# Delta-rule attention followed by a mixture of experts: group preparation, expert 0's first slots and expert 1's split moved in the order

## Chip, cores and metric

The kernel runs on one core of a Trainium2 chip. The metric is the device time of one launch in microseconds (us), as the median of runs; the time before is 915.78 us, of 3 runs. The program has two halves that follow one another: attention, in 24 units, and a mixture of 8 experts.

## What is computed

The first half is a recurrence over 768 steps for each of 4 x 8 heads, with a 40 x 40 state; the second sends each of the 3072 rows of its result to 2 of 8 experts. Cut to what matters:

```python
for t in range(S):                                   # 768 steps, state 40 x 40 per head
    y[:, :, t] = einsum('bhd,bhde->bhe', rt, state)
    Sa = einsum('bhde,bhe->bhd', state, at)
    state = state * wt - einsum('bhd,bhe->bhde', Sa, bt) + einsum('bhd,bhe->bhde', vt, kt)
x = y as 3072 rows of 320
noisy = x @ w_gate + log1p(exp(x @ w_noise)) * noise  # 3072 x 8
top2, top2_w = the two largest of 8, softmax over the two
for e in range(8):                                   # w1[e] is 320 x 1024, w2[e] is 1024 x 320
    out[rows of e] += weight * (relu(x[rows of e] @ w1[e]) @ w2[e])
```

## The kernel before

**Attention.** The 768 steps are cut into 12 chunks of 64; half of the batch (p = 0 or 1) in one chunk is a unit, so 24 units, each of which writes one tile of 128 rows (`run`, `for n in range(N+1)`). Four units with two chunks form a group g (units 4g to 4g+3). Before a group can run, it is prepared, inside the units of the groups before it (`prep`): loads of w, a and k/b (`loadw`, `loada`, `loadq`), a scan on DVE with its logarithm and exponential on ACT (`scan`, `lnexp`), the factor NH on DVE (`newton`), products on POOL that write A (`mula`, am) and KB (`mulk`, bm and km), 64 matmuls and an eviction (`prepS`, L: tiles lt and No; `prepK`, K: tile ak), transposes of KB (`quad`). lt goes to DRAM (scr) by `flush`, comes back as X (`Solve`), POOL solves 16 x 16 triangles in it in 14 pairs of operations on X and Tt (`step`), it is written to DRAM again (`done`) and comes back as XD (`fetchD`, fD), in two chunks. A table of events (`ev(unit, slot, function)`) says in which unit and in which slot of the unit's body each step is issued; `do(n,slot)` issues them.

A unit's body is a chain that PE runs through in order: pkb of the unit before (tile YS), xdt (pX, from XD), state (pd, WS), mm1, the last unit's result (pg), umm, mmx (px) three times with DVE's H and dT between, ut (pU), rmm (sc from RV, VU; DVE writes PV), akv, rnmm. All compute instructions of this half go through a wrapper that chains each engine's instructions in program order, so their line in the profile is L443, the wrapper's. DMAs of SP are chained likewise. Every engine takes its queue in order: an instruction that waits holds all behind it.

**Route.** The rows' logits come with pg (DVE's lg). After 8, 8, 4, 2 and 2 tiles (`RTS`) a generator `route` computes the gate, ranks and slots in small steps; each of the six `adv` calls of a unit runs one step and one scatter (POOL's indirect DMA ls<-ent,po, one for each tile and rank). cnt on DVE feeds pr on PE (counts of rows before), pr feeds po, the slots. Rows of the first `NA` = 20 tiles go to the list ls[0] and the rows xd[0], later ones to copies ls[1], xd[1]; `turn` copies the list.

**Experts.** An expert has 832 slots in two parts (`PARTS`): 0 to 511, filled from the first 20 tiles for expert 0, and 512 to 831. `loadx` reads the list of a part (le, by SP) and gathers rows (xr, POOL's indirect DMA per 128 rows), `trans` turns them on PE (pt) and splits them into two f16 halves (xh on ACT, xl and x3l on DVE), `split1` and `split2` do so with the weights (w1h, w1l, w2h, w2l), `hidden` makes 8 blocks of 8 matmuls (ph; hh on ACT, hl on DVE), `output` 24 matmuls for each 128 slots (po; y on ACT), which POOL adds to the output. `sized` and `finite` are reductions on DVE (mx, yc) for a flag. For the experts the order comes from a scheduler, except where `pin` sets an operation behind another of the same engine (`marks`); the splits of expert 0 are pinned to places in the units, those of expert 1 behind the last instruction of the units (`s.end`), and mx<-xr is free.

Of the kernel before, what the change touches and what calls it, by code (L numbers as in the profile page):

```python
# [17 lines left out]
R=104  # L18
# [4 lines left out]
NA=20  # L23
# [8 lines left out]
PARTS=((0,512),(512,CAP-512))  # L32
# [12 lines left out]
class Moe:  # L45
# [81 lines left out]
    def route(s,n0,T,lg):  # L127
# [9 lines left out]
        yield 1  # L137
        pr=s.rps[0].tile([128,T,8],F32,name="pr",tag=s.rps[1],bufs=s.rps[2])
# [146 lines left out]
    def trans(s,x,e,X=None,part=0):  # L285

        nc=s.nc; xp=s.xps[e%2]
        if X is None:
            X=[xp.tile([128,2,s.cap],F16,name="xh"),xp.tile([128,2,s.cap],F16,name="xl"),
               xp.tile([128,s.cap],F16,name="x3"),xp.tile([128,s.cap],F16,name="x3l")]  # L290
        xh,xl,x3,x3l=X
        t0,n=s.parts[part]; t0%=CAP
        for k in range(3):
            pt=s.pt.tile([128,512],F32,name="pt",bufs=2)
            f0=min(128*k,DM-128)
            for t,p in tiles(t0,n): nc.tensor.transpose(pt[:,t-t0:t-t0+p],x[:p,t//128,f0:f0+128],s.idm[:p,:p])  # L296
            r=slice(t0,t0+n)
            if k<2:
                nc.scalar.activation(xh[:,k,r],pt[:,:n],AF.Copy,scale=XE)  # L299
                nc.vector.scalar_tensor_tensor(xl[:,k,r],pt[:,:n],XE,xh[:,k,r],op0=ALU.mult,op1=ALU.subtract)  # L300
            else:
                for q in (slice(0,64),slice(64,128)): nc.scalar.activation(x3[q,r],pt[64:128,:n],AF.Copy,scale=XE)
                for q in (slice(0,64),slice(64,128)): nc.vector.scalar_tensor_tensor(x3l[q,r],pt[64:128,:n],XE,x3[64:128,r],op0=ALU.mult,op1=ALU.subtract)
        return X
    def hidden(s,W,X,part):
        nc=s.nc; wh,wl=W; xh,xl,x3,x3l=X
        t0,n=s.parts[part]; t0%=CAP; r=slice(t0,t0+n)
        hh=s.hp.tile([128,8,n],F16,name=f"hh{part}"); hl=s.hp.tile([128,8,n],F16,name=f"hl{part}")
        for f in range(8):
# [170 lines left out]
class Att:  # L480
    def __init__(s,nc,tc,ctx,aps):
# [5 lines left out]
        s.No=[own(f"No{i}",[128,2,CG*4,64]) for i in range(4)]; s.XDT=own("XDT",[128,8,64])  # L487
        s.ak=[own(f"ak{i}",[128,2,CG*4,64]) for i in range(2)]
        s.MT=own("MT",[128,2,4,64]); s.XD=[own(f"XD{i}",[128,4,2,2,64]) for i in range(2)]; s.H1=own("H1",[128,2,4,64]); s.H2=own("H2",[128,2,4,64])
        s.A=[own(f"A{(i+2*NG)%SAB}",[128,NS,64]) for i in range(SAB)]; s.A=[s.A[(i-2*NG)%SAB] for i in range(SAB)]  # L490
        s.Gx=[own(f"Gx{i}",[R,NS,64]) for i in range(SAB)]; s.ge=[own(f"ge{i}",[R,NS,1]) for i in range(SAB)]
        s.kbt=[own(f"kbt{i}",[128,CG*640+24]) for i in range(4)]
# [206 lines left out]
    def run(s,m,xo=None):  # L699
# [62 lines left out]
        def prep(g):  # L762
# [10 lines left out]
            ev(n-7,'f1',lambda: (scan(g,0),am(g,0)))  # L773
            ev(n-7,'a1',lambda: ln(g,0)); ev(n-7,'a2',lambda: ex(g,0))
# [10 lines left out]
            ev(n-3,'f1',lambda: sol[g].step(Pl,15))  # L785
            ev(n-2,'f2',lambda: done(g,Pl))
# [3 lines left out]
        def finish(o,n):  # L790
            xt,lg=s.rows(o)
            if m is not None: m.logits(n,xt,lg)
            else: nc.sync.dma_start(xo[o['p'],o['cc']],xt)
        for n in range(N+1):
# [41 lines left out]
            do(n,'s3')  # L836
# [133 lines left out]
```

## Time and profile before

| | us |
|---|---|
| median of 3 runs | 915.78 |
| lowest, highest | 911.03, 918.65 |
| the profiled execution, its own time | 919.16 |
| its span, first to last instruction | 917.4 |
| PE busy | 771.6 (84%) |
| DVE, POOL, ACT busy | 485.5, 383.4, 332.8 |

Times in the profile count from the start of the span. A row of the timeline has start, length, engine, line, operation, out<-in, shapes, the count of merged instructions, and in brackets how long the engine sat idle before and what ended that. PE is matmuls, PEld its weight loads, SPq the queue of SP that issues DMAs. A row of the windows has the stretch, its length, busy time and count of PE, PEld, DVE, ACT and POOL, then the mean granted TensorE clock (1.0 is 2.4 GHz, 0.5 is 1.2 GHz), the share of the DMA engines and GB/s. In the list of waits stand total us, times, longest. Unit 4 begins at about 146 us, unit 23 at about 490 us, the experts behind 514 us.

### The profile page before, as it was taken

What the parts mean: (1) busy time and instruction counts of PE and PEld (TensorE: products, weight loads), DVE (VectorE), ACT (ScalarE), POOL (GpSimd) and SP (SyncE); (2) the same over time, 40 slices, a digit from 0 to 9 for tenths busy, and PEclk for the clock granted to TensorE, in tenths of its full rate; (3) what the DMA queues carried; (4) which work ended last, traced back from release to release, by engine and by line L of the source; (5) the groups of instructions that cost most, each with busy time, mean ns of one, the idle gap of its engine ahead of it and who ended that gap; (6) DMA issues with size and microseconds to landing.
All of it is one profiled execution on the core that took longest, in us unless ns stands there. A gap on an engine that the chain in (4) does not pass through costs nothing.

```text
span 917.4 us, 28566 instructions
## 1 busy us (share of the span) xinstructions
PE 771.6 (84%) x12521; PEld 591.7 (65%) x12521; DVE 485.5 (53%) x959; ACT 332.8 (36%) x684; POOL 383.4 (42%) x496
## 2 busy tenths in 40 slices
PE   0063798998798998898984599999999999999994
PEld 0043687887787887787873346566666666666663
DVE  6372464654674654653563754775656565654231
ACT  3021343443343442342432324544444353533230
POOL 9031453263279563256223337525251526141313
PEclk9985898999898997999897589999999999999997
DMA  8942364755765764657595325717171717130303
GB/s 156 187 88 58 82 153 115 159 146 137 186 159 102 150 161 93 165 126 173 131 266 151 105 59 108 192 50 185 27 189 21 191 27 183 38 41 8 40 9 44
DMA packets 164393, 106.81 MB, mean 116 GB/s; under 512 B 116847, under 2 KB 147443, under 8 KB 163971
## 3 DMA queue, kind: packets, MB, share of 16 engines
q1 hardware_dynamic: 152099, 87.75, 39.1%
q0 software_dynamic: 12160, 17.15, 10.8%
q8 instruction: 100, 1.64, 0.8%
q14 instruction: 34, 0.28, 0.1%
HBM read 80.16 MB, written 28.10 MB: 118 GB/s over the span
## 4 chain that ended last, share of the span: by engine, by line
PE 65%; DMA 11%; POOL 10%; DVE 5%; issue 4%; SPq 3%; ACT 1%; POOLq 0%; ACTq 0%
PE ph L314 20%; PE po L328 19%; PE sc L443 6%; PE YS L443 6%; PE px L443 4%; POOL X L443 3%; PE WS L443 3%; PE pt L296 2%; DMA scr<-X 2%; PE pg L443 2%; DMA scr<-lt 2%; SPq L443 2%; POOL Tt L443 2%; DMA X<-scr 2%; DMA XD<-scr 2%
## 5 line engine op out<-in xcount | busy, mean ns | idle before, releaser
L337 POOL DMA_INDIRECT out_dram<-y,le x48 | 80.0, 1667 | 183.0 <-ACT y L331 180.2
L316 DVE SCALAR_TENSOR_TENSOR hl<-ph,hh 128x320 f16<-128x320 f32 (+1 forms) x128 | 74.6, 589 | 72.1 <-ACT hh L315 71.1
L315 ACT ACTIVATE hh<-ph 128x320 f16<-128x320 f32 (+1 forms) x128 | 65.6, 516 | 127.2 <-PE ph L314 125.7
L314 PEld LDWEIGHTS <-w1h 128*128 128x128 f16 x768 | 74.4, 99 | 57.4 <-issue 6.1
L328 PEld LDWEIGHTS <-hh 128*128 128x128 f16 (+1 forms) x1024 | 84.2, 101 | 37.0 <-issue 3.7
L443 POOL TENSOR_TENSOR KB<-KB,NH 104x1024 f32<-104x1024 f32 x20 | 47.5, 2399 | 99.9 <-DMA KB<-in_fm_dram 56.6
L443 PE MATMUL sc<-A,KB 64*64 64x64 f32 x1536 | 34.6, 245 | 53.1 <-DVE mk L511 20.0
L328 PE MATMUL po<-w2h,hh 128*128 128x320 f16 (+1 forms) x512 | 74.3, 284 | 0.2 <-ACT hh L315 0.2
L283 POOL DMA_INDIRECT xr<-xd,le x56 | 54.3, 969 | 36.4 <-DMA le<-ls 17.1
L314 PE MATMUL ph<-xh,w1h 128*128 128x512 f16 (+1 forms) x256 | 66.8, 345 | 3.1 <-ACT xh L299 3.1
L328 PE MATMUL po<-w2h,hl 128*128 128x320 f16 (+1 forms) x512 | 68.3, 282 | 0.0
L328 PE MATMUL po<-w2l,hh 128*128 128x320 f16 (+1 forms) x512 | 67.7, 282 | 0.0
L314 PE MATMUL ph<-xh,w1l 128*128 128x512 f16 (+1 forms) x256 | 67.2, 343 | 0.0
L314 PE MATMUL ph<-xl,w1h 128*128 128x512 f16 (+1 forms) x256 | 66.6, 342 | 0.0
L443 PEld LDWEIGHTS sc<-A,KB 64*64 64x64 f32 x1536 | 30.9, 156 | 54.4 <-issue 26.5
L443 DVE TENSOR_TENSOR H<-px,XD 128x512 f32<-128x512 f32 x48 | 33.2, 691 | 61.8 <-PE px L443 61.0
L331 ACT ACTIVATE y<-po,le 128x320 f32<-128x320 f32 (+1 forms) x56 | 28.3, 505 | 87.6 <-PE po L328 87.6
L227 DVE TENSOR_REDUCE yc<-y 128x1 f32<-128x320 f32 (+1 forms) x56 | 25.3, 460 | 54.9 <-ACT y L331 54.6
L443 POOL DMA_INDIRECT ls<-ent,po x44 | 47.9, 1088 | 9.5 <-issue 8.0
L328 PEld LDWEIGHTS <-hl 128*128 128x128 f16 (+1 forms) x512 | 42.4, 101 | 14.6
L443 PE MATMUL sc<-RV,VU 64*128 64x64 f32 x768 | 50.2, 282 | 0.9 <-ACT VU L443 0.7
L443 ACT ACTIVATE kbt<-ptr 128x320 f32<-128x320 f32 x48 | 20.9, 436 | 82.4 <-PE ptr L443 82.4
(261 smaller groups left out, 1591.9 us busy)
## 6 DMA issues: line engine op xcount, KB each, us to landing
w2r<-in_w_dram SPq DMA_DIRECT2D x7, 1280.0 KB
w1r<-in_w_dram SPq DMA_DIRECT2D x7, 1024.0 KB
KB<-in_fm_dram SPq DMA_DIRECT2D x32, 208.0 KB
w1r<-in_w_dram SPq DMA_DIRECT2D x20, 256.0 KB
RV<-in_rv_dram SPq DMA_DIRECT2D x24, 208.0 KB
VU<-in_rv_dram SPq DMA_DIRECT2D x24, 208.0 KB
V<-in_vt_dram SPq DMA_DIRECT2D x24, 160.0 KB
PV<-in_vt_dram SPq DMA_DIRECT2D x48, 80.0 KB
```

Source lines behind the costliest of these rows:

```text
L227: s.pin(s.nc.vector.tensor_reduce(s.yc[q:128,s.ny:s.ny+1],a,axis=AX.X,op=ALU.add),0); s.ny+=1
L283: for k in range(c,c+a): nc.gpsimd.indirect_dma_start(out=x[:p,k],out_offset=None,in_=s.xd[w],in_offset=OFFS(ap=li[:p,k,0:1],axis=0))
L296: for t,p in tiles(t0,n): nc.tensor.transpose(pt[:,t-t0:t-t0+p],x[:p,t//128,f0:f0+128],s.idm[:p,:p])
L314: for i,(a,b) in enumerate(mm): nc.tensor.matmul(ph[:,:n],a,b,start=i==0,stop=i==7)
L315: nc.scalar.activation(hh[:,f],ph[:,:n],AF.Relu)
L316: nc.vector.scalar_tensor_tensor(hl[:,f],ph[:,:n],0.0,hh[:,f],op0=ALU.max,op1=ALU.subtract)
L328: for j in range(c): nc.tensor.matmul(po[p*j:p*j+p,:d],h[:,f,r],w[:,f,d*j:d*j+d],start=k==0,stop=k==23)
L331: nc.scalar.activation(y[:,:d],po[:,:d],AF.Copy,scale=w_[:,ii:ii+1])
L337: st=nc.gpsimd.indirect_dma_start(out=o_,out_offset=OFFS(ap=ix,axis=0),in_=yv,in_offset=None,compute_op=ALU.add)
L443: i=f(*a,**kw)
```

## The change

1. The preparation of groups 2 to 5 is moved: the loads are packed into fewer units (six slots, s0 to s5); L stands in a new slot `L` behind the result of the last unit, its eviction and `flush` right behind it; NH, bm and km of the first half at the end of unit 4g-6, of the second at the end of unit 4g-5; the solver's load and its steps in unit 4g-4, `done` at the end of unit 4g-3; scan and NH stand behind the first mmx or at the unit's end, not at its start. fD goes from behind the third mmx to the unit's start from unit 4 on. Group 1 keeps its slots.
2. `route` has one more step between cnt and pr.
3. `NA` is 16 and part 0 has 384 slots, part 1 has 448. The list and rows of expert 0's part 0 are read in unit 20 (`early`), turned and split in units 22 and 23 (`trans1`), into tiles of their own.
4. mx<-xr, the reductions of expert 0's w1l and w1h, and expert 1's splits of w1 are pinned behind the last route's po (`s.placed`) and between the hh and hl of expert 0.
5. Some tiles change places in SBUF.

```diff
-NA=20
+NA=16
-PARTS=((0,512),(512,CAP-512))
+PARTS=((0,384),(384,CAP-384))
...
         cnt=r("cnt",dt=F16); nc.vector.tensor_tensor(cnt,oh[:,:,0],oh[:,:,1],op=ALU.add)
         yield 1
+        yield 1
...
-        s.mark(8); s.finite(l.rearrange("p k f->p (k f)")); s.mark(10); s.finite(h[64:128,2],64)
+        s.w1=lambda: (s.mark(8),s.finite(l.rearrange("p k f->p (k f)")),s.mark(10),s.finite(h[64:128,2],64))
+        if e: s.w1()
...
+    def early(s):
+        n=PARTS[0][1]//128; l=s.kp.tile([128,n,4],F32,name="le0"); x=s.kp.tile([128,n,DM],F32,name="xr0")
+        li=l.rearrange("p a f->p (a f)").bitcast(I32).rearrange("p (a f)->p a f",a=n)
+        s.x0=s.loadx(0,(x,l[:,:,2],li[:,:,1:2],l,li),0); s.X0=s.xtiles(s.kp,PARTS[0][1],"0")
...
         with s.tc.high_priority(offset=PX):
-            x=s.loadx(0); W1=s.split1(r1,0); X=s.trans(x[0],0)
-            s.sized(x[0][:,0])
-        W2=s.split2(r2,0); H0=s.hidden(W1,X,0)
+            W1=s.split1(r1,0)
+        W2=s.split2(r2,0); H0=s.hidden(W1,s.X0,0); hm=s.hm
...
             H1=s.hidden(W1,X,1)
+            if e==0: s.at=s.placed,; s.sized(s.x0[0][:,0]); s.marks=[s.at]*12; s.w1(); s.at=None; s.marks=[(s.placed,hm[k][1]) for k in (4,4,5,5,6,6,7,7,7,7,7,7)]+[s.hm[k] for k in (2,2,3,3,4,4)]
...
-                for u,l in ((n-8,(None,w_(0,0),w_(0,1),la(0,0))),(n-7,(la(0,1),w_(1,0),w_(1,1),lq(0,0))),
-                            (n-6,(lq(0,1),lq(0,2),lq(0,3),la(1,0))),(n-5,(la(1,1),lq(1,0),lq(1,1),lq(1,2))),(n-4,(lq(1,3),))):
+                for u,l in ((n-8,(w_(0,0),w_(0,1),la(0,0),la(0,1),w_(1,0),w_(1,1))),(n-7,(None,)*5+(lq(0,0),)),
+                            (n-6,(lq(0,1),lq(0,2),lq(0,3),la(1,0),la(1,1),lq(1,0))),(n-5,(lq(1,1),lq(1,2),lq(1,3)))):
...
-            ev(n-6,'f1',lambda: nh(g,0))
-            ev(n-5,'f1',lambda: (bm(g,0),km(g,0),scan(g,1)))
-            ev(n-5,'f2',lambda: am(g,1))
-            ev(n-5,'a1',lambda: ln(g,1)); ev(n-5,'a2',lambda: ex(g,1))
-            ev(n-5,'sc',lambda: L(g,0))
-            ev(n-4,'f1',lambda: (nh(g,1),bm(g,1),km(g,1)))
-            ev(n-4,'sc',lambda: L(g,1)); ev(n-3,'ld2',lambda: sol_(g))
+                ev(n-6,'f1',lambda: nh(g,0)); ev(n-6,'p4',lambda: (bm(g,0),km(g,0)))
+                ev(n-5,'L',lambda: L(g,0)); ev(n-5,'fl',s.flush)
+                ev(n-5,'f1',lambda: (scan(g,1),am(g,1)))
+                ev(n-5,'p2',lambda: ln(g,1)); ev(n-5,'a1',lambda: ex(g,1))
+                ev(n-5,'p4',lambda: (nh(g,1),bm(g,1),km(g,1)))
+                ev(n-4,'L',lambda: L(g,1)); ev(n-4,'fl',s.flush)
+                ev(n-4,'p3',lambda: sol_(g)); ev(n-4,'p4',lambda: sol[g].step(Pl,15))
+                ev(n-3,'p4',lambda: done(g,Pl))
...
-            ev(n-3,'f1',lambda: sol[g].step(Pl,15))
-            ev(n-2,'f2',lambda: done(g,Pl))
...
+        def late(n): return n<6
...
+            if not late(n+2): fD(n+2)
...
+                if n==EX: m.early()
+                if n==EX+2: m.trans1(m.x0[0],m.X0,0,0,s.ps,"pB",1)
+                if n==EX+3: m.trans1(m.x0[0],m.X0,0,2,s.ps,"pB",1)
...
+            if m is not None and n==EX+2: m.trans1(m.x0[0],m.X0,0,1,s.ps,"pA",1)
...
+EX=20
```

On SP's queue, the last group's way from X to XD, before:

```order
L443 DMA X<-scr 128x1024
L443 DMA PV_266<-in_vt_dram 64x8x40 x2
L443 DMA xd_651<-xt 128x320
L443 DMA RV_261<-in_rv_dram 104x512
L443 DMA VU_263<-in_rv_dram 104x8x64
L443 DMA V_264<-in_vt_dram 128x320
L443 DMA PV_267<-in_vt_dram 64x8x40 x2
L443 DMA xd_651<-xt 128x320
L443 DMA scr_6143<-X 128x1024
L443 DMA XD_133<-scr_6143 32x16x32 x4
```

The same on SP's queue in the changed kernel (xd is the row store, RV, VU, V and PV are the inputs of later units):

```order
L450 DMA X<-scr 128x1024
L450 DMA RV_260<-in_rv_dram 104x512
L450 DMA VU_262<-in_rv_dram 104x8x64
L450 DMA V_265<-in_vt_dram 128x320
L450 DMA PV_266<-in_vt_dram 64x8x40 x2
L450 DMA xd_652<-xt 128x320
L450 DMA scr_5900<-X 128x1024
L450 DMA RV_261<-in_rv_dram 104x512
L450 DMA VU_263<-in_rv_dram 104x8x64
L450 DMA V_264<-in_vt_dram 128x320
L450 DMA PV_267<-in_vt_dram 64x8x40 x2
L450 DMA XD_209<-scr_5900 32x16x32 x4
```

X is read one set of a unit's inputs earlier, and the solved block is written and read back with a set between, where XD followed the write at once.

On DVE's queue in unit 23, before, from the gate's wq to cnt:

```order
L443 TENSOR_TENSOR wq<-l_7261 128x2
L224 TENSOR_REDUCE mx<-xr 128x1
L443 TENSOR_TENSOR PV_267<-sc,mk 128x8x64 x2
L443 TENSOR_SCALAR wq<-wq 128x2
L443 RECIPROCAL ent<-wq 128x2
L443 TENSOR_TENSOR ent<-wq,ent 128x2
L443 CAST xf<-ix 128x4
L443 TENSOR_TENSOR oh<-io,xf 128x32
L443 TENSOR_SCALAR ent<-ent 128x4
L443 TENSOR_TENSOR cnt<-oh 128x16
```

The same place on DVE in the changed kernel (x3l is the third split of expert 0's part 0):

```order
L450 TENSOR_TENSOR PV_267<-sc,mk 128x8x64 x2
L450 SCALAR_TENSOR_TENSOR x3l_6708<-pt,x_6707 64x384 x2
L450 TENSOR_SCALAR wq<-wq 128x2
L450 RECIPROCAL ent<-wq 128x2
L450 TENSOR_TENSOR ent<-wq,ent 128x2
L450 CAST xf<-ix 128x4
L450 TENSOR_TENSOR oh<-io,xf 128x32
L450 TENSOR_SCALAR ent<-ent 128x4
L450 TENSOR_TENSOR cnt<-oh 128x16
```

The reduction mx<-xr is gone from there, two x3l have come.

On PE where the units end, before (pg is the last unit's result, pt the transposes of expert 0):

```order
L443 MATMUL pg<-IW,yT 128x120 x4
L296 MATMUL pt<-idm,xr 128x128 x8
L314 LDWEIGHTS w1h
L314 MATMUL ph<-xh,w1h 128x512
L314 LDWEIGHTS w1h
L314 MATMUL ph<-xh,w1h 128x512
```

The same on PE in the changed kernel:

```order
L450 MATMUL pg<-IW,yT 128x120 x4
L321 LDWEIGHTS w1h
L321 MATMUL ph<-xh_6705,w1h 128x384
L321 LDWEIGHTS w1h
L321 MATMUL ph<-xh_6705,w1h 128x384
L321 LDWEIGHTS w1h
```

The first hidden matmuls follow pg without a transpose between.

## Rows read from the trace of the kernel before

**Rows 1.** Page, part 2: PE busy tenths and granted TensorE clock in 40 slices.

```profile
PE   0063798998798998898984599999999999999994
...
PEclk9985898999898997999897589999999999999997
```

**Rows 2.** Chain of waits, the experts: start us, length us, what, instructions.

```profile
797.98 16.72 PE po L328 x158
...
844.83 16.72 PE po L328 x158
861.55 5.29 PE ph L314 x24
...
890.00 15.52 PE po L328 x149
```

**Rows 3.** Windows: three units, full and slowed; columns as in the section above.

```profile
247.20:264.60 17.40, 17.20 (x421) 15.63 (x421) 12.36 (x49) 7.50 (x17) 7.69 (x20) 0.84 0.55 136
264.60:279.80 15.20, 14.45 (x414) 13.04 (x412) 9.22 (x22) 5.19 (x13) 13.31 (x27) 1.00 0.71 162
279.80:300.40 20.60, 16.66 (x414) 14.90 (x412) 8.70 (x18) 8.21 (x17) 19.14 (x21) 0.83 0.46 96
```

**Rows 4.** List of waits of PE, 90 to 515 us, then timeline of PE.

```profile
PE pX L443 <- DMA XD<-scr: 14.9, 5, 4.2
...
145.55 0.63 PE L443 MATMUL pX<-idf,XD 128*128 128x128 f32 x4 [2.98 <-DMA XD<-scr]
...
247.19 1.09 PE L443 MATMUL pX<-idf,XD 128*128 128x128 f32 x4 [4.17 <-DMA XD<-scr]
```

**Rows 5.** Timeline of PE: single waits in units 11, 14 and 21.

```profile
293.21 1.11 PE L443 MATMUL ptr<-idf,KB 128*128 128x128 f32 x4 [3.72 <-POOL KB L443]
...
338.23 0.60 PE L443 MATMUL pU<-idf,Up 128*128 128x128 f32 x4 [1.58 <-DVE H L443]
...
467.79 0.19 PE L443 MATMUL pr<-cnt,tri 128*128 128x32 f16 x1 [2.95 <-DVE cnt L443]
```

**Rows 6.** Timeline of unit 23: the gather, its reader, pr and pg.

```profile
500.26 0.99 POOL L283 DMA_INDIRECT xr<-xd,le  x1 [11.80 <-DMA le<-ls]
...
504.05 0.48 DVE L224 TENSOR_REDUCE mx<-xr 128x1 f32<-128x320 f32 x1 [11.76 <-DMA xr<-xd,le]
...
506.78 0.20 PE L443 MATMUL pr<-cnt,tri 128*128 128x16 f16 x1 [10.92 <-DVE cnt L443]
...
511.89 2.06 PE L443 MATMUL pg<-IW,yT 104*128 104x120 f32 x8 [0.78 <-DVE yT L443]
```

**Rows 7.** Timeline from the last pg to part 1's first gather.

```profile
514.43 2.95 ACT L253 ACTIVATE w1h<-w1r 128x1024 f16<-128x1024 f32 x3
...
519.89 2.72 PE L314 MATMUL ph<-xh,w1h 128*128 128x512 f16 x6 [3.07 <-ACT xh L299]
...
537.84 0.16 DVE L156 SCALAR_TENSOR_TENSOR po<-pf,junk 128x4 int32<-128x4 f32 x1
...
542.14 0.97 POOL L167 DMA_INDIRECT ls<-ent,po  x1 [0.30 <-issue]
...
546.62 0.99 POOL L283 DMA_INDIRECT xr<-xd,le  x1 [3.51 <-DMA le<-ls]
```

**Rows 8.** Timeline: DVE's split and reduction, and a scatter beside them.

```profile
517.00 1.21 DVE L254 SCALAR_TENSOR_TENSOR w1l<-w1r,w1h 128x1024 f16<-128x1024 f32 x1
517.08 2.00 POOL L443 DMA_INDIRECT ls<-ent,po  x1 [0.16 <-issue]
...
520.38 2.28 DVE L227 TENSOR_REDUCE yc<-w1l 128x1 f32<-128x2048 f16 x1
```

**Rows 9.** Timeline: third gather of part 1 and its transposes.

```profile
549.19 0.93 POOL L283 DMA_INDIRECT xr<-xd,le  x1 [0.30 <-issue]
...
553.69 1.16 PE L296 MATMUL pt<-idm,xr 128*128 128x128 f32 x6
```

**Rows 10.** Page, part 5: the products that POOL writes to KB.

```profile
L443 POOL TENSOR_TENSOR KB<-KB,NH 104x1024 f32<-104x1024 f32 x20 | 47.5, 2399 | 99.9 <-DMA KB<-in_fm_dram 56.6
```

More of the change, by code (lines that the diff above doesn't have):

```diff
@@ L267, in split2 @@
         s.mark(17); s.sized(w[:,0])
-        s.at=None; s.marks=[s.end]*18 if e==0 else []
+        s.at=None; s.marks=[]
         return h,l
@@ L287, in trans @@
         nc=s.nc; xp=s.xps[e%2]
[L288 to L291, printed above, removed]
-        t0,n=s.parts[part]; t0%=CAP
[L293 to L303, printed above, removed]
@@ L304, in trans, with xtiles, trans1 @@
-        return X
+        if X is None: X=s.xtiles(xp,s.cap,"")
+        for k in range(3): s.trans1(x,X,part,k,s.pt,"pt",2)
+        return X
+    def xtiles(s,xp,n,z):
+        return [xp.tile([128,2,n],F16,name="xh"+z),xp.tile([128,2,n],F16,name="xl"+z),xp.tile([128,n],F16,name="x3"+z),xp.tile([128,n],F16,name="x3l"+z)]
+    def trans1(s,x,X,part,k,pool,tag,bufs):
+        nc=s.nc; xh,xl,x3,x3l=X
+        t0,n=s.parts[part]; t0%=CAP
+        pt=pool.tile([128,512],F32,name="pt",tag=tag,bufs=bufs)
+        f0=min(128*k,DM-128)
+        for t,p in tiles(t0,n): nc.tensor.transpose(pt[:,t-t0:t-t0+p],x[:p,t//128,f0:f0+128],s.idm[:p,:p])
+        r=slice(t0,t0+n)
+        if k<2:
+            nc.scalar.activation(xh[:,k,r],pt[:,:n],AF.Copy,scale=XE)
+            nc.vector.scalar_tensor_tensor(xl[:,k,r],pt[:,:n],XE,xh[:,k,r],op0=ALU.mult,op1=ALU.subtract)
+        else:
+            for q in (slice(0,64),slice(64,128)): nc.scalar.activation(x3[q,r],pt[64:128,:n],AF.Copy,scale=XE)
+            for q in (slice(0,64),slice(64,128)): nc.vector.scalar_tensor_tensor(x3l[q,r],pt[64:128,:n],XE,x3[64:128,r],op0=ALU.mult,op1=ALU.subtract)
@@ L486, in __init__, with pair, five @@
         s.KB=[own(f"KB{i}",[128,NS,2,64]) for i in range(2)]
[L487 removed]
+        s.No,s.kbt,s.A,s.Gx,s.ge={},{},{},{},{}
+        def pair(i): s.No[i]=own(f"No{i}",[128,2,CG*4,64]); s.kbt[i]=own(f"kbt{i}",[128,CG*640+24])
+        def five(i): s.A[i]=own(f"A{i}",[128,NS,64]); s.Gx[i]=own(f"Gx{i}",[R,NS,64]); s.ge[i]=own(f"ge{i}",[R,NS,1])
+        l=2*((NG-1)%2); z=[(2*NG-2+p)%SAB for p in range(2)]
+        for i in range(4):
+            if i//2*2!=l: pair(i)
+        for i in range(2,SAB): five((i+z[0])%SAB)
+        for i in range(2): pair(l+i)
+        for i in z: five(i)
+        s.No,s.kbt=[[d[i] for i in range(4)] for d in (s.No,s.kbt)]; s.A,s.Gx,s.ge=[[d[i] for i in range(SAB)] for d in (s.A,s.Gx,s.ge)]
+        s.XDT=own("XDT",[128,8,64])
         s.ak=[own(f"ak{i}",[128,2,CG*4,64]) for i in range(2)]
         s.MT=own("MT",[128,2,4,64]); s.XD=[own(f"XD{i}",[128,4,2,2,64]) for i in range(2)]; s.H1=own("H1",[128,2,4,64]); s.H2=own("H2",[128,2,4,64])
[L490 to L492 removed]
         s.wk=ec(tc.tile_pool(name="wk",bufs=2))
@@ L793, in finish, with ld @@
             else: nc.sync.dma_start(xo[o['p'],o['cc']],xt)
+        def late(n): return n<6
+        def ld(n,k):
+            for i in do(n,'s%d'%k):
+                if k in (2,3,4): s.tc.add_manual_dep(i.ins,nc.scalar.last,mybir.DependencyInfo(mybir.DependencyClass.Sync,mybir.DependencyReason.DATA),reason="pace")
         for n in range(N+1):
@@ L802, in run @@
                 finish(r,n-1)
-                if m is not None: m.scatter(99); m.end=(V.last,nc.scalar.last)
+                if m is not None: m.scatter(99); m.end=(V.last,nc.scalar.last,nc.tensor.last)
                 break
             G=Gof(n); first=o['cc']==0; w1=s.w1[n%2]; x=O[n+1] if n+1<N else None
-            do(n,'f1'); adv(1)
+            adv(1)
             s.unit(o,G)
@@ L817, in run @@
             if x: s.mmx(x,0)
+            for f in z: f()
+            do(n,'f1')
             s.ut(o)
+            ld(n,2); do(n,'p2')
             adv(1)
@@ L822, in run @@
             s.rmm(o)
+            do(n,'f3')
             adv(0)
             if x: s.akv(x,Gof(n+1))
+            ld(n,3); do(n,'p3')
             do(n,'a1'); do(n,'qa',"pB"); do(n,'a2')
+            if m is not None:
+                if n==EX: m.early()
+                if n==EX+2: m.trans1(m.x0[0],m.X0,0,0,s.ps,"pB",1)
+                if n==EX+3: m.trans1(m.x0[0],m.X0,0,2,s.ps,"pB",1)
             adv(1)
-            if x: s.mmx(x,2); fD(n+2)
-            for i in do(n,'s2'): s.tc.add_manual_dep(i.ins,nc.scalar.last,mybir.DependencyInfo(mybir.DependencyClass.Sync,mybir.DependencyReason.DATA),reason="pace")
+            if x: s.mmx(x,2)
+            if late(n+2): fD(n+2)
+            ld(n,4); do(n,'p4')
             z=do(n,'sc')
```

31 lines of the change are left out of this document (18 added, 13 removed).

## Prediction

> **What bounds the kernel now.** Start with the slices of the page: the granted clock stays near full except for a hollow in the 22nd to 24th slice (481 to 550 us), where the two halves of the program meet [rows 1]. Behind it PE is full to the end: from expert to expert the chain of waits steps by 844.83-797.98 = 46.85 us [rows 2], 8 x 46.85 = 374.8 us for all experts, and nothing in the change shortens an expert. So I read the units (90 to 514 us) and the meeting point. In the units PE is also the bound: a unit with the clock at 1.00 takes 15.2 us [rows 3], and the losses are single waits. The list of waits has 14.9 us in 5 waits for XD, the solved blocks that come back from DRAM [rows 4]. The first, 2.98 us at 145.55, belongs to group 1; the largest, 4.17 us, is at 247.19. Behind such a wait the unit runs at a mean granted clock of 0.84 (the two levels are 1.2 and 2.4 GHz, 0.5 and 1.0 of the scale) and takes 17.4 us instead of 15.2, so it costs 2.2 us more. A wait of 3.72 us for KB, which POOL writes too late, is at 293.21, and that unit takes 20.6 us; 2.95 us for cnt at 467.79 [rows 3, 5].
>
> In unit 23 PE waits 10.92 us for cnt [rows 6]. DVE had nothing hard to do: the reduction mx<-xr stands in its queue ahead of PV and cnt, and sat until 504.05 for the gather that started at 500.26 (3.8 us from a gather's start to its first reader). The last pg ends at 511.89+2.06 = 513.95. From there to the last po, 890.00+15.52 = 905.52 [rows 2], are 391.6 us, 16.8 more than the 374.8 of PE's work: expert 0 waits for its transposes, splits and the clock [rows 7].
>
> **The change, part by part.**
>
> XD waits. For groups 2 to 5 L of the second half, the flush, the solver's load and done all move one to two slots earlier, and XD is issued at a unit's start instead of behind its third mmx, half a unit (7 us) sooner. Waits of at most 4.17 us then go, with the margin: 14.9-2.98 = 11.9 us. Their clock: 2.2 us at the largest, half of that at two others, 4.4 us. Together **-16.3**; bounds 0 (the loads' burst, below, eats the margin) and -16.3.
>
> KB. bm and km of the first half go from the start of unit 4g-5 to the end of the unit before; the transposes of KB that waited come 9 us later. -3.72, and of the unit's 20.6 us another 20.6-15.2-3.72 = 1.7: **-5.4**. Bounds 0 and -5.4.
>
> Route. pr gets one more step, and the 2.28 us reduction yc<-w1l [rows 8], which stood ahead of cnt in unit 21, goes behind the last route: **-2.95** of 2.95, at worst 0.
>
> Unit 23. mx<-xr goes behind the last route: -10.92. From pr at 506.78 to the end of pg took 7.2 us at the low clock; without it I estimate 4.9 (the rows of pr, YS and pg with PE's times halved, yT's wait kept): -2.3. New there: three transposes of part 2, and x3l twice in DVE's queue ahead of cnt. PE has about 1.1 us of work between rmm and pr; PV, x3l and the small operations take DVE some 3.9 us: +2.8. **-10.4**; bounds -13.2 and -5.
>
> Added in the units. Nine transposes: six at full clock took 1.16 us [rows 9], so 1.7; their evictions hold pA and pB, which the next px and pr want, 1.0 (0 to 3): **+2.7**. The gather for them waits on POOL and its list on SP in unit 20; behind that list in SP's queue stand RV and VU of unit 22, a unit and a half before use, which hides a wait of up to about 20 us; uncovered it would be one wait like those above. NH now stands ahead of yT on DVE, so Sst and pg may come late; H behind the same operations let PE wait 1.58 us at 338.23 [rows 5]. Four groups at half of that: **+3.2** (0 to 6.3). Six pieces of a group's loads now leave in one unit, three or four before; group 1's chain is not moved, so its wait of 2.98 stays and may grow: **+1.5** (0 to 3).
>
> The meeting point. Part 0 is gathered, turned and split before the last pg, so ph can follow it at once; split1 of expert 1 (three ACT operations at 514.43, 2.95 us, which held xh and the route's u) stands behind the last route. The work ahead is smaller too. A ph of 512 columns takes 5.29/24 = 0.22 us [rows 2], of 384 an estimated 0.165: hidden 64 x 0.165 = 10.6, output 72 x 0.13 (the 320-column share of the same) = 9.6: 20.2 us of PE's work before part 1's transposes stand in its queue, where 26 stood before. What is late next is part 1: last route, four scatters, list, gathers. Before, po came at 537.84, 23.9 us behind pg, held by DVE and ACT work of expert 1 that is now behind it. I count from the end of pg: lg and the gate's 20 small operations at 0.1 to 0.2 us with three hl between them, cnt at 5.6; pr behind five ph groups on PE, 7.2; ten more operations and two hl, po at 10. From there by rows: the last scatter's end, 542.14+0.97 = 543.11, is 5.3 behind po, the first gather 546.62-543.11 = 3.5 later, the fourth 3 x 1.3 later, 3.8 to its reader: 26.5. Then transposes and their evictions that no matmul covers, and 6 ph of the low clock: PE is 10.2 us behind its 374.8, against 16.8 before. Transposes moved out of it: -1.0. So -7.6, with bounds of -17.8 (the whole loss and the 1.0 go) and +5 (the chain as slow as before). One row speaks against even this: a scatter at 517.08 took 2.00 us beside w1l instead of 0.97 [rows 7, 8], and w1l, w1l, w1h now stand right behind po, beside the four scatters. One hit, +1.0: **-6.6**.
>
> On this the Trainium skill (SBUF — State Buffer, section Who interferes with whom) says that a DVE operation with two SBUF inputs and a GpSimd operation that reads SBUF shut each other out for the whole instruction. The trace agrees for that scatter; 2.00 us is too short to show which of the two waited. By the rule all three splits could hit, 3.6 us instead of 1.0 by the row, and the forecast below would be 884.
>
> Sum: -16.3-5.4-2.95-10.4-6.6 = -41.7, +7.4 added: **-34.3**. The profiled execution took 919.16 us (917.4 of span, 1.8 around it), 3.4 above the median of 915.78; from its own time I come to 884.9, from the median to 881.5. I predict **881** for the median.
>
> **The rivals.** *The chain is hidden* (0.18). If DVE brings po at 7 and the gathers land faster than the 3.8 us row, part 1 is there when output 0 ends. For it: third gather to transpose took 553.69-549.19 = 4.5 with PE busy, so nobody saw the true landing [rows 9]. Against it: DVE is also to split w1l. The loss of 16.8 goes but for 2: 915.78-34.3-8 = 873, or 868 with every wait of the units gone.
>
> *The units keep their waits* (0.22), the form in which the change does not do what it says. The moved loads meet scr<-lt and X<-scr of the group before, and XD is as late as now; the KB wait only changes place. Then -16.3 and -5.4 fall out: 915.78-34.3+21.7 = 903; half of it is 892. For it: the largest XD wait, at 247.19, was for a block solved long before, so SP's queue and the DMA queues made it late, not the solver. Against it: SP now issues it 7 us sooner.
>
> *Slower: L waits for POOL* (0.04). L of the second half now stands in the first third of unit 4g-4, where NH and KB have been issued only at the end of the unit before: about 7 us of PE's work, the last third of the unit and the start of the next, cover POOL's 2.40 us for bm [rows 10] and NH ahead of it on DVE, three operations on the same tile, taken at as much. Where POOL is behind its scatters, PE waits at each L: 4 groups x 2 halves at the price of the KB wait with its clock, 5.4 us, are 43 us, against 34 gained: 924. It decides from 4.3 us a time on. Against it: without scatters POOL is idle there, and scatters run in only two of the four groups.
>
> **How the numbers follow.** Forecast 0.56, own range 872 to 890; hidden 0.18 at 868 to 873; waits kept 0.22 at 892 to 903; slower 0.04. The range of 862 to 900 leaves out the upper end of the waits kept, the slower case, and little below. A measurement of this kernel tells about 1% from no change, here 9 us: faster needs under 906.6, which the first three cases give but for a tail of the third: faster 0.91, same 0.05, slower 0.04.
>
> **What would show it.** No PE wait for XD behind unit 4 and a mean unit of about 15.2; no wait for KB above 1 us; unit 23 shorter by 10 us, with a wait of about 3 us for cnt left; ph right behind the last pg; po of the last route about 10 us behind it; a PE wait of some 3 to 6 us before part 1's transposes; the step from expert to expert still 46.85. The forecast is wrong if XD or KB waits stand in units 5 to 19, if SP's wait for the list in unit 20 lets rmm of unit 22 wait, or if expert 0 loses more than 14 us.

## Result and the profile after

The changed kernel takes 906.4 us in the median of 20 runs, beside 916.1 of before: a ratio of 0.9915 [0.9888, 0.9943], so 8 to 10 us came where 34 were predicted. Some executions of each kernel are over 1.5% longer than its fastest; the ratios leave them out, and where the traced execution was such a one (e3, f4 and h3 below) the table of the experiments gives no stages. The profiled execution of the changed kernel took 904.97 us, with a span of 903.3. The stages of the two traces, read from the first pX in a unit's body, the last pg and the last po (us), follow. Counted so, unit 4 of the kernel before begins at 163 us, not at 146 as stated above, which is unit 3.

| stage | before | after | difference | predicted |
|---|---|---|---|---|
| start to unit 0 | 100.1 | 102.9 | +2.8 | 0 |
| units 0 to 21 | 371.9 | 369.0 | -2.9 | -20.0 |
| unit 22 to the last pg's end | 42.0 | 31.1 | -10.9 | -7.7 |
| last pg to last po | 391.6 | 387.6 | -4.0 | -6.6 |
| last po to the end | 11.9 | 12.7 | +0.8 | 0 |
| span | 917.4 | 903.3 | -14.1 | -34.3 |

In the last column the nine transposes (+2.7) stand where they run, in units 22 and 23. The two traced executions lie 14.1 us apart, more than the medians; the runs of after alone scatter from 899 to 920. The slices of PE and of the granted clock on the page of after, to be held against [rows 1]:

```profile
PE   0054698998987898899787969999999999999994
...
PEclk9995699999999999989889979999999999999997
```

The hollow of the 22nd to 24th slice has narrowed to the 24th, where the clock is at 0.7, and from the sixth slice to there it is at 0.8 or more. So the units should be faster. That they are not shows in PE's list of waits, 90 to 515 us (total us, times, longest), where the 14.9 us for XD of [rows 4] are now 2.9:

```profile
PE sc L450 <- POOL KB L450: 12.2, 3, 5.7
PE px L450 <- issue: 6.3, 6, 1.6
PE YS L450 <- DVE dT L450: 4.9, 11, 1.5
PE sc L450 <- issue: 4.1, 4, 1.8
PE YS L450 <- issue: 3.5, 4, 1.3
PE pU L450 <- issue: 3.2, 2, 2.9
PE pX L450 <- DMA XD<-scr: 2.9, 1, 2.9
PE pr L450 <- DVE cnt L450: 2.7, 1, 2.7
```

The waits that name "issue", so nothing that the profile sees, have come in place of XD's. From 100 us to unit 22 they are 18.8 us, before 6.7: 12.1 more, and XD 12.0 less. I call them gaps. Those of 0.45 us and more stand, but for one, in the middle of a run of equal matmuls:

```profile
376.39 0.21 PE L450 MATMUL px<-XD,MT 64*64 64x64 f32 x1 [1.57 <-issue]
...
442.64 0.55 PE L450 MATMUL pU<-idf,Up 128*128 128x128 f32 x3 [2.87 <-issue]
```

The DMA view of the second gap, 439.77 to 442.64 us, in 40 slices, says what PE waited for:

```profile
DMA  9789969789965454121100000000100000001688
...
q1 hardware_dynamic: 1233, 0.16, 44.0%
q8 instruction: 1, 0.02, 2.4%
```

The DMA engines are full in the first third (XD and xd), a block of 16 KB comes on the instruction queue (440.01 to 441.13 us), then almost nothing moves, and PE resumes 1.50 us behind the block's landing. The trace has 17 gaps of 0.45 us and more between unit 0 and unit 22; 16 of them end 1.27 to 1.62 us behind such a landing. Of the 72 blocks from 100 to 490 us, the 16 that end a gap were preceded by 3 us in which the engines were 99% busy (the packets' time, added up); before the other 56 it was 54%. So I read q8 as PE's instructions: they come through the same DMA engines as the loads, and where these are full, they can come late. It is not a rule: 12 of the other 56 blocks also had engines that were 90% busy or more ahead of them, and no gap of that size ended behind them.

### The profile page after: what moved, and what is told of

Its sections match the earlier page's. It is cut to its first block, busy times and chain, and to the rows that moved or that the text cites. A ratio compares the mean times of both kernels' runs of the same rounds, so it can differ in the third digit from the quotient of the medians.

```text
span 903.3 us, 28574 instructions
## 1 busy us (share of the span) xinstructions
PE 766.6 (85%) x12521; PEld 585.8 (65%) x12521; DVE 488.4 (54%) x959; ACT 333.4 (37%) x684; POOL 382.9 (42%) x496
## 3 DMA queue, kind: packets, MB, share of 16 engines
q0 software_dynamic: 12160, 17.15, 10.9%
## 5 line engine op out<-in xcount | busy, mean ns | idle before, releaser
L323 DVE SCALAR_TENSOR_TENSOR hl<-ph,hh 128x448 f16<-128x448 f32 (+1 forms) x128 | 73.5, 587 | 72.3 <-ACT hh L322 71.6
L322 ACT ACTIVATE hh<-ph 128x448 f16<-128x448 f32 (+1 forms) x128 | 65.6, 517 | 124.1 <-PE ph L321 122.2
L450 PEld LDWEIGHTS sc<-A,KB 64*64 64x64 f32 x1536 | 31.1, 159 | 64.0 <-issue 30.3
L335 PE MATMUL po<-w2l,hh 128*128 128x320 f16 (+1 forms) x512 | 69.6, 286 | 0.0
L321 PE MATMUL ph<-xh,w1h 128*128 128x384 f16 (+1 forms) x256 | 66.9, 345 | 0.9 <-ACT xh L303 0.5
L321 PE MATMUL ph<-xh,w1l 128*128 128x384 f16 (+1 forms) x256 | 66.3, 339 | 0.0
L321 PE MATMUL ph<-xl,w1h 128*128 128x384 f16 (+1 forms) x256 | 65.9, 339 | 0.0
L285 POOL DMA_INDIRECT xr<-xd,le x53 | 51.8, 978 | 25.3 <-issue 17.8
L450 POOL DMA_INDIRECT ls<-ent,po x44 | 45.4, 1032 | 11.8 <-issue 11.0
L450 PEld LDWEIGHTS sc<-RV,VU 64*128 64x128 f32 x768 | 47.5, 194 | 3.8 <-issue 1.3
```

The costliest lines, as they stand in the source:

```text
L285: for k in range(c,c+a): nc.gpsimd.indirect_dma_start(out=x[:p,k],out_offset=None,in_=s.xd[w],in_offset=OFFS(ap=li[:p,k,0:1],axis=0))
L321: for i,(a,b) in enumerate(mm): nc.tensor.matmul(ph[:,:n],a,b,start=i==0,stop=i==7)
L322: i=nc.scalar.activation(hh[:,f],ph[:,:n],AF.Relu)
L323: s.hm+=[(nc.vector.scalar_tensor_tensor(hl[:,f],ph[:,:n],0.0,hh[:,f],op0=ALU.max,op1=ALU.subtract).ins.name,i.ins.name)]
L335: for j in range(c): nc.tensor.matmul(po[p*j:p*j+p,:d],h[:,f,r],w[:,f,d*j:d*j+d],start=k==0,stop=k==23)
L450: i=f(*a,**kw)
```

## The experiments

The runs of one letter ran beside each other on one chip; the chips differ, and the kernel before took 916 to 948 us on them, so each ratio is against before beside the same letter's runs. "Gaps" and "XD" are PE's idle us for issue and for XD from unit 0 to unit 22. Not all gaps end 1.1 to 1.8 us behind a block: in the traces of e, f and g 8 to 10 us of them, mostly short ones, do not (f1: 8.3 of its 13.9 us, f2: 10.1 of 22.6); in the first pair that is under 1 us, in those of h and k nothing. Of k1 one run can be compared; before took 920.9 us beside it.

| run | ratio [95%] | unit 0 at | units 0 to 21 | gaps | XD |
|---|---|---|---|---|---|
| e1 moe only | 0.9971 [0.9925, 1.0016] | 104.7 | 389.4 | 14.9 | 18.5 |
| e2 prep only | 0.9865 [0.9810, 0.9919] | 99.1 | 381.0 | 22.5 | 3.9 |
| e3 XD late | 0.9938 [0.9896, 0.9979] | | | | |
| e4 loads spread | 0.9757 [0.9669, 0.9844] | 103.7 | 380.1 | 20.8 | 3.3 |
| f1 before | 0.9990 [0.9950, 1.0029] | 99.0 | 388.5 | 13.9 | 15.5 |
| f2 changed | 0.9894 [0.9839, 0.9949] | 103.5 | 384.4 | 22.6 | 3.6 |
| f3 loads twice | 0.9947 [0.9914, 0.9980] | 103.8 | 392.9 | 28.5 | 3.2 |
| f4 loads spread | 0.9801 [0.9739, 0.9862] | | | | |
| g1 clear later | 0.9815 [0.9766, 0.9865] | 99.2 | 379.0 | 22.7 | 3.1 |
| g2 V in mid-unit | 0.9905 [0.9863, 0.9946] | 105.1 | 379.9 | 21.1 | 4.9 |
| g3 XD in mid-unit | 0.9968 [0.9924, 1.0011] | 104.8 | 393.2 | 28.2 | 5.2 |
| g4 three edits | 0.9813 [0.9760, 0.9866] | 100.0 | 372.9 | 24.2 | 1.7 |
| h1 loads less | 0.9722 [0.9654, 0.9791] | 104.3 | 351.8 | 7.9 | 1.4 |
| h2 loads none | 0.9698 [0.9629, 0.9767] | 103.9 | 344.1 | 7.1 | 1.3 |
| h3 changed | 0.9815 [0.9745, 0.9886] | | | | |
| h4 clear and spread | 0.9785 [0.9739, 0.9832] | 99.7 | 362.6 | 11.4 | 6.0 |
| k1 before, loads none | (889.6 us) | 100.7 | 341.9 | 9.6 | 2.9 |
| k2 changed, loads none | 0.9602 [0.9501, 0.9704] | 103.0 | 340.9 | 3.8 | 1.7 |

**The halves.** e1 puts the preparation back, e2 is before with the preparation alone, e3 takes back XD's place only:

```diff
-        def late(n): return n<6
+        def late(n): return True
```

> The changed kernel with the preparation table, the slots and XD of the kernel before; the route's extra step, NA=16, part 0 in 384 slots, the early gather and transposes and the pinned reductions and splits stay. Theory A (the preparation's gain was eaten inside the units, the boundary did its work): the two traces put the boundary at 10.9 us for unit 23 and 4.0 us behind the last pg, less 1.7 us of transposes, so 903 us here (900 to 906), at or below the changed kernel's 906.4; XD waits of 10 to 15 us are back. Theory B (both halves gave about half of what came): 911 us.

> The kernel before with only the new preparation table, its slots, XD at the unit's start and the tiles' new places in SBUF; list, parts, gathers, reductions and splits as before. Theory A: XD waits behind unit 4 are gone, but issue gaps of PE of 15 to 20 us stand in the units; 913 to 917 us, no gain. Theory B: 911 us. My recorded prediction's terms (16.3+5.4 less 4.7) would give 899 us.

> The changed kernel with XD issued behind the third mmx in all units, as before. Theory A (PE gets back as gaps without a releaser what it saves at XD): pX waits of 5 to 15 us come back, issue gaps from 90 to 490 us fall from 19 to 10 us or less, time within 4 us of the changed kernel, 903 to 910. Rival (the gaps have another cause, and an early XD is worth its waits): the gaps stay near 19 us and the time rises by the waits, to 914 to 920.

Theory A fails in this form. e1 gained little, and its unit 0 starts 5.7 us later than that of f1 (another chip, but 947 and 946 us for before). e2 gained 1.4%, not nothing: its units took 7.5 us less than f1's, and unit 23 is shorter too, though mx<-xr was not pinned there. The scheduler put it behind the last pg by itself once the instructions around it had moved, and the wait for cnt fell from 10.92 to 2.38 us:

```profile
506.86 0.20 PE L443 MATMUL pr<-cnt,tri 128*128 128x16 f16 x1 [2.38 <-DVE cnt L443]
```

So the halves do not add up term by term. e3's ratio is above that of the changed kernel elsewhere (0.989, 0.9915, 0.9815): that points to some worth of an early XD, more than theory A allows, but across chips. In e3's one trace, which the table leaves out, the waits for XD are back (16.6 us) and the gaps have not fallen (23.5 us): as far as it goes, that is the rival and not theory A.

**The loads' order.** e4 and f4 spread a group's 16 loads, f3 adds a transfer:

```diff
-                for u,l in ((n-8,(w_(0,0),w_(0,1),la(0,0),la(0,1),w_(1,0),w_(1,1))),(n-7,(None,)*5+(lq(0,0),)),
-                            (n-6,(lq(0,1),lq(0,2),lq(0,3),la(1,0),la(1,1),lq(1,0))),(n-5,(lq(1,1),lq(1,2),lq(1,3)))):
+                for u,l in ((n-8,(w_(0,0),w_(0,1),None,la(0,0),None,la(0,1))),(n-7,(w_(1,0),None,None,w_(1,1),None,lq(0,0))),
+                            (n-6,(lq(0,1),lq(0,2),lq(0,3),la(1,0),None,la(1,1))),(n-5,(lq(1,0),lq(1,1),lq(1,2),lq(1,3)))):
...
+        if o['n']>1: s.nc.sync.dma_start(s.dup[o['n']%2],F[:,0:1024])
```

> The changed kernel with a group's 16 loads spread over its four units as 4, 3, 5, 4 instead of 6, 1, 6, 3. Theory C (the packed loads make the gaps): issue gaps fall below 10 us, time 896 to 900. Theory A (the gaps come with PE's own pace, not with the loads): gaps stay within 15 to 22 us, time 904 to 909; a late load may add a KB or A wait of 1 to 3 us.

> The kernel before, unchanged, for a trace from the same chip as its neighbours. All theories: ratio 1. Theory A (PE's instructions, read from DRAM in blocks of 16 KB beside the loads, come late where the DMA engines are full; a kernel with fewer waits meets that more often): issue gaps of PE in the units of 5 to 12 us. Rival (the gaps belong to the chip and the run, not to the kernel): as many as in the changed kernel on this chip, within 4 us.

> The changed kernel, unchanged, timed and traced beside the others. Theory A: ratio 0.985 to 0.995, issue gaps of 15 to 22 us in the units, each of 0.45 us and more ending 1.2 to 1.7 us behind the landing of a block on the instruction queue. Rival: the first call's chip had ratios of 0.997 and 0.987 for the two halves, whose product is 0.984.

> The changed kernel with one more transfer in every unit, RV's and VU's 416 KB copied to scratch in DRAM that nobody reads; PE, DVE, ACT and POOL do the same work. Theory A: issue gaps rise from about 19 to 30 us or more and the time by 10 us or more. Rival (PE outruns its supply by its own pace, whatever the loads do): gaps stay within 4 us, time within 5 us. A third way: XD or KB land late, seen as waits that name a DMA.

> The changed kernel with a group's 16 loads spread as 4, 3, 5, 4 over its four units, as in the first call, where it had the lowest ratio to before, 0.976, but no changed kernel beside it. If the spread helps: 5 to 10 us below the changed kernel of this call. If it does nothing: within 4 us of it.

Spreading left the gaps at 20.8 us, so theory C falls as the cause of the gaps; its ratios were lower beside both befores (e4, f4), but h4, with the clearing of g1 moved as well, is only 0.003 below h3, inside the intervals. One more transfer in each unit raised the gaps by 5.9 us and units 0 to 21 by 8.5: the direction of theory A, at half the size that I had named; the ratios of f3 and f2 overlap. f1 and f2, on one chip, repeat the exchange of the first pair: XD -11.9, gaps +8.7, of which 6.9 end behind a block. I had expected every gap of 0.45 us and more in f2 to end 1.2 to 1.7 us behind a block; 10 of 15 do, in f1 4 of 10.

**Three remedies.** g1 takes xd's clearing out of the start, g2 moves V and PV, g3 moves XD, g4 joins g1, g2 and the spread:

```diff
-        n=24-NA; nc.sync.dma_start(s.xd[0][128*NA:3072].rearrange("(p a) (h d)->p (a h) d",p=128,h=2),z.rearrange("p (o d)->p o d",o=1).to_broadcast([128,2*n,DM//2]))
...
+            if m is not None and 14<=n<18: m.clear(n-14)
...
-            s.flush(); do(n,'ld'); fV(n+2); do(n,'ld2')
+            s.flush(); do(n,'ld'); do(n,'ld2')
...
             do(n,'f2')
+            fV(n+2)
+            if n: fA(n+1)
...
+            if not late(n+2): fD(n+2)
             ld(n,2); do(n,'p2')
```

> The changed kernel, but the clearing of xd's later rows (1280 KB since NA is 16, 640 KB before) leaves the start and is issued in four pieces at the ends of units 14 to 17. Theory (it stands on SP and on the DMA engines ahead of scr<-lt, whose way through DRAM the first unit waits for): the first pX comes at 75 to 78 us instead of 81 to 83, the ratio to before falls by 0.004 to 0.007 against the changed kernel's 0.989 to 0.992. Rival (the start's delay has another cause): first pX stays at 81 us.

> The changed kernel with V's and PV's loads issued in the middle of a unit (behind the second mmx) instead of at its start, where XD now follows them. Theory (the burst RV, VU, V, PV, XD at a unit's start makes PE's instruction block late): issue gaps from u0 to u22 fall from 19 to 23 us to 13 or less, ratio 0.980 to 0.986. Rival (any busy stretch does it, the same bytes only move): gaps stay at 18 or more, ratio 0.989 to 0.992.

> The changed kernel with XD issued behind the first mmx of a unit: some 5 us behind V and PV, and some 5 us sooner than before the change. Theory of the burst at the unit's start: gaps fall to 15 or less, XD waits behind unit 4 stay under 4 us in all, ratio 0.982 to 0.988. Rival (XD has to be at the start, or the gaps are not its): XD waits of 5 us and more come back, or gaps stay at 18 or more; ratio 0.989 or above.

> The changed kernel with the loads spread (4, 3, 5, 4), the clearing moved out of the start and V and PV in mid-unit. If the three add up: spread 0.976 and 0.980 in two calls, less 0.005 for the start and 0.004 to 0.008 for the gaps, so a ratio of 0.965 to 0.972. If the spread and V's place are one and the same remedy: 0.973 to 0.977.

g1 shows a part of the change that I had overlooked. Line 98 clears xd's rows from NA on; the diff does not touch it, but NA=16 makes it 1280 KB instead of 640. It stands on SP ahead of scr<-lt, the first chunk's way through DRAM. SP's queue and POOL's first use of X, before and then after (the number in brackets is POOL's wait):

```profile
35.08 3.79 SPq L597 DMA_DIRECT2D scr<-lt  x4
...
51.09 0.34 SPq L459 DMA_DIRECT2D X<-scr  x1
```

```profile
37.38 2.96 SPq L611 DMA_DIRECT2D scr<-lt  x4
...
52.75 0.34 SPq L466 DMA_DIRECT2D X<-scr  x1
...
56.27 1.27 POOL L450 TENSOR_SCALAR_AFFINE_SELECT X<-X 128x1024 f32<-128x1024 f32 x1 [33.38 <-DMA X<-scr]
```

The first pX of after, and of g1:

```profile
81.19 1.09 PE L450 MATMUL pX<-idf,XD 128*128 128x128 f32 x4 [8.97 <-DMA XD<-scr]
```

```profile
77.77 1.09 PE L451 MATMUL pX<-idf,XD 128*128 128x128 f32 x4 [11.38 <-DMA XD<-scr]
```

With the clearing moved, unit 0 starts at 99.2 us (g4: 100.0), on the same chip as g2 and g3, which keep the clearing and start at 105.1 and 104.8. g2 and g3 moved bytes within the unit and took no gap away (21.1 and 28.2 us, g1 22.7): the burst at the unit's start is not it, and g4 is no better than g1.

**The bytes.** h1 leaves out RV's and VU's loads from the third unit on, h2, k1 and k2 those of V and PV too. PE's instructions stay the same:

```diff
+        if o['n']>1: return
```

> The changed kernel without RV's and VU's loads from the third unit on (the first two units' values are used again, so the results differ; 416 KB a unit less). Transfers make the gaps: issue gaps from u0 to u22 fall from 19 to 23 us to 15 to 18, u0 to u22 shorter by 5 to 10 us than in the changed kernel of this call. PE's pace makes them: gaps within 3 us of that kernel's.

> As before it, and V's and PV's loads left out too (736 KB a unit less; the results differ). Transfers make the gaps: 12 us or less, u0 to u22 shorter by 10 to 20 us with the clock that the gaps cost. PE's pace makes them: gaps within 3 us of the changed kernel's, u0 to u22 within 5.

> The changed kernel, unchanged, as the level for the others of this call: first pX at 81 to 83 us, gaps 19 to 23 us, ratio 0.985 to 0.995.

> The changed kernel with xd's clearing out of the start and the loads spread (4, 3, 5, 4), V and PV left at the unit's start. If the spread is worth the 0.010 to 0.014 that it showed beside the changed kernel: 0.968 to 0.976. If that was the scatter between runs: 0.979 to 0.985, like the moved clearing alone.

> The kernel before without V's, PV's, RV's and VU's loads from the third unit on (results differ). If the XD waits belong to the order of the preparation: 9 to 15 us of pX waits stay, and u0 to u22 is 10 to 20 us longer than in the next run, the gain that I had predicted for the units. If they were late transfers: pX waits of 4 us or less, u0 to u22 within 5 us of the next run.

> The changed kernel without the same loads, on the same chip: u0 to u22 at 344 us (340 to 350), issue gaps 6 to 9 us, pX waits of 3 us or less behind unit 4.

These runs decide it for the gaps. The windows of units 0 to 21, with columns as in [rows 3]: before, after, h1 and h2.

```profile
100.09:471.96 371.87, 331.51 (x8728) 297.88 (x8728) 206.19 (x434) 141.75 (x325) 174.66 (x269) 0.93 0.62 146
```

```profile
102.88:471.87 368.99, 329.39 (x8728) 293.51 (x8728) 208.69 (x431) 142.07 (x325) 176.50 (x268) 0.96 0.64 146
```

```profile
104.26:456.01 351.75, 325.90 (x8728) 290.65 (x8728) 209.62 (x431) 142.19 (x325) 175.34 (x270) 0.96 0.54 131
```

```profile
103.92:447.99 344.07, 318.94 (x8727) 284.15 (x8728) 211.41 (x431) 142.10 (x325) 176.00 (x269) 0.98 0.43 110
```

PE issues the same 8728 (in one trace 8727) matmuls, and with the DMA share at 0.43 instead of 0.64 it is through 25 us sooner, at a higher clock. The gaps fall to 7.9 us in h1 already, where I had expected 15 to 18, and to 7.1 in h2. k1 and k2 ask what the order is worth without these loads. Kernel before, then the changed one, both without these loads:

```profile
100.69:442.57 341.88, 315.52 (x8728) 283.44 (x8728) 214.53 (x434) 141.54 (x325) 175.35 (x269) 0.98 0.43 115
```

```profile
103.00:443.89 340.89, 317.26 (x8728) 282.32 (x8728) 209.61 (x431) 142.00 (x325) 174.42 (x269) 0.99 0.44 111
```

And the line for XD in the list of waits of k1, 90 to 490 us:

```profile
PE pX L443 <- DMA XD<-scr: 2.9, 3, 1.5
```

In the old order, with XD issued behind the third mmx, the waits for XD fall from 14.9 to 2.9 us without these loads, and the units take 341.9 us against 340.9 in the new order. k1's units also hold a wait of 2.5 us for cnt that k2's route avoids, so without these loads the new order of the preparation gains nothing (one trace of each).

The waits for XD that the change removed were thus made by these loads. How is shown in part. Leaving them out frees the DMA engines, and it also takes transfers out of SP's queue, in which RV's stood before for a buffer that PE's YS had to free. SP's list of waits of before, 100 to 472 us, has them; that of k1 has none:

```profile
SPq L443 <- PE YS L443: 40.6, 18, 8.9
```

For the XD of 247.19 us it was the engines: SP had issued the last of its parts at 240.15, and up to its landing they were 96% busy. At 211.59 and 349.11 POOL had ended the solve only 6.5 and 7.2 us ahead, after it had waited for X up to 189.5 and 326.5; whether SP's queue or the engines held X up, no run separates.

## Why the prediction was wrong

The failing step is the one of the **XD waits** (-16.3). The waits went as said (14.9 to 2.9), and their time did not come out. I read PE as the bound of the units, and the waits as a matter of where XD is issued, with PE's work as what is left once they are gone. The runs show that the loads hold the units: without V, PV, RV and VU the waits for XD go in the old order too (k1), and the gaps in which PE's instructions are late fall from 18.8 to 7.1 us (h2). With the loads there, PE's idle time in the units went only from 40.4 to 39.6 us (371.87-331.51, 368.99-329.39): XD gave 12.0, and the gaps took 12.1. That the one makes the other is not shown; e3 speaks against it.

The clock that I priced with the waits did rise, from 0.93 to 0.96, but PE's busy time fell by 2.1 us only. By an estimate from the windows, busy time times granted clock, the same matmuls took more work time in the new order: 308 and 316 us in the first pair, 319 and 321 in f1 and f2, 309 and 314 in k1 and k2. No run says why.

The signs were in the rows: a share of the DMA engines of 0.46 to 0.71 in [rows 3], and the remark in my own rival that the block at 247.19 had been solved long before. I gave that rival, *the units keep their waits*, 0.22, and its price for half of the waits, 892, to its full one, 903; the median is 906. Its mechanism was near (transfers late, and the wait for KB did only change place), its form was not: XD's own wait did go.

**KB** (-5.4): the waits of 3.72 and 1.26 us did not go, L has them now, behind bm and km on POOL, 2.87 and 3.58 us in units 11 and 12. That is the slower rival, twice instead of eight times. On the chip of f1 and f2 neither trace has more than 0.8 us of waits for KB in these units, so the term was read from one trace's wait.

```profile
288.39 1.16 PE L450 MATMUL sc<-A,KB 64*64 64x64 f32 x64 [2.87 <-POOL KB L450]
...
307.12 1.98 PE L450 MATMUL sc<-A,KB 64*64 64x64 f32 x64 [3.58 <-POOL KB L450]
```

**Route** (-2.95): right; unit 21 has no wait for cnt. **Unit 23** (-10.4): right in its mechanism. From its first pd (488.75 and 487.05 us) to the end of pg it took 25.2 us and takes 16.0, so -9.2, three of the transposes included. Unit 22 became 1.6 us shorter with the other six, because a wait of 2.77 us of YS shrank to 0.93, which no term had; each three transposes took 0.55 us, near the 1.7 for nine. The wait for cnt that was to be new, 2.8 us, measures 2.72, and the last pg ends at 503.01:

```profile
497.94 0.18 PE L450 MATMUL pr<-cnt,tri 128*128 128x16 f16 x1 [2.72 <-DVE cnt L450]
501.86 1.15 PE L450 MATMUL pg<-IW,yT 104*128 104x120 f32 x8 [0.79 <-DVE yT L450]
```

**Added in the units**: YS waits 4.9 us for dT instead of 2.0; that is near the 3.2 for NH. The **start** (+2.8) was missing from the sum: NA also sets the size of a transfer on a line that the diff leaves alone.

**Meeting point** (-6.6, measured -4.0): ph follows pg at once, po comes 9.1 us behind pg (predicted 10), and one scatter takes 1.78 us instead of 0.97, the one hit that I counted. But the splits did not stand right behind po, as I had said: the reductions mx and yc ran first, and only the last of the four scatters met a split:

```profile
516.02 1.23 DVE L255 SCALAR_TENSOR_TENSOR w1l<-w1r,w1h 128x1024 f16<-128x1024 f32 x1
516.31 1.78 POOL L168 DMA_INDIRECT ls<-ent,po  x1 [0.31 <-issue]
```

So the size of that term came out by luck, and three hits by the rule of the Trainium skill that I weighed there (SBUF — State Buffer, section Who interferes with whom) were not put to the test. The one meeting agrees with the rule: the split that had begun first kept its 1.23 us, and the scatter took 0.8 longer than the three before it (0.97 to 1.01). What was too small is the gathers' landing:

```profile
524.44 0.96 POOL L285 DMA_INDIRECT xr<-xd,le  x1 [0.30 <-issue]
525.71 0.92 POOL L285 DMA_INDIRECT xr<-xd,le  x1 [0.30 <-issue]
...
529.82 0.33 PE L300 MATMUL pt<-idm,xr 128*128 128x128 f32 x1 [2.52 <-DMA xr<-xd,le]
...
532.92 0.48 PE L300 MATMUL pt<-idm,xr 128*128 128x128 f32 x1 [2.78 <-DMA xr<-xd,le]
```

The fourth gather starts 22.7 us behind pg, as I had counted (26.5 less 3.8). But the transposes wait at 529.82 for the second and at 532.92 for the third, which had started at 523.16 and 524.44: 6.7 and 8.5 us instead of the 3.8 that I took from a single gather in unit 23. From 523.16 to 532.92 the DMA engines were 97% busy, with w1r and the gathers of expert 1 on the queues; beside that single gather it was 83%.

In sum the units miss 17.1 us, the start 2.8, the meeting point 2.6 and the tail 0.8, and units 22 and 23 gave 3.2 more. The sign of the forecast and its two terms from DVE's order (route, unit 23) held; they and the meeting point are the gain.

The version with the clearing moved is under before on both chips where it ran (0.9815 and, with the spread, 0.9785) and starts its units 3 to 4 us sooner than the changed kernel; beside that kernel (0.9815, h3) the intervals overlap, so it is not shown to be faster as a whole. Left open is why the gaps of the old order, 7 to 15 us, were fewer than the 19 to 28 of the new one under the same loads: I did not separate the waits that hide a late block from the denser work of PE.

## What to carry to other kernels

The time of a wait for a transfer comes back only if nothing else that PE needs is late for the same reason. Where a block that was ready long ago still lands late (here with a DMA share of 0.62 over the units), count the bytes of the stage first. To test that, leave loads out of both kernels: here two runs showed that without them the old order took 341.9 us and the new one 340.9. And look for every line that uses a constant which the diff changes, not only for the changed lines.

## What the runs showed of the hardware

PE's instructions arrive in blocks of 16 KB through the DMA engines that carry the loads. On the page of after they are the row q8, 100 packets, one for every 250 of PE's 25042 matmuls and weight loads; that they are PE's is read from the gaps that end behind them:

```profile
q1 hardware_dynamic: 153091, 87.75, 41.0%
q0 software_dynamic: 12160, 17.15, 10.9%
q8 instruction: 100, 1.64, 0.8%
```

With the engines full ahead of a block, PE can stand still in the middle of a run of equal matmuls, in after for up to 2.87 us, and goes on 1.3 to 1.6 us behind the landing. The list of waits calls this "issue". Such a gap can also cost clock. The windows of after's unit 17, with a gap of 1.57 us at 394.09, and of unit 18, without one:

```profile
385.88:405.63 19.75, 17.98 (x424) 16.09 (x422) 11.92 (x49) 5.40 (x14) 12.73 (x39) 0.83 0.45 111
405.63:420.33 14.70, 14.50 (x414) 13.06 (x413) 6.50 (x18) 5.18 (x13) 6.73 (x12) 1.00 0.65 149
```

Of the 5.05 us between them the gap itself is a third. Of the 17 gaps of 0.45 us and more only this one and the one of 2.87 us had a stretch at half clock right behind them; another of 1.57 us, at 376.39, had none. Without V, PV, RV and VU, 736 KB of some 2.4 MB in a unit (146 GB/s over 16.8 us), both kernels run their units at a granted clock of 0.98 and 0.99, instead of 0.93 and 0.96.
